# A planned attention stage: costs and delays of the plan set anew, GpSimd and VectorE kept apart in it, one chain of squarings on ScalarE

## The chip, the cores and the metric

The kernel runs on one core of a Trainium2 chip. The metric is the device time of one execution in microseconds, the median of several runs. The engines are TensorE (PE in the rows; PEld is its loading of weights), VectorE (DVE), ScalarE (ACT), GpSimd (POOL) and SyncE (SP), whose queue issues most DMAs. Each engine works through its own queue in order and waits on semaphores for the others.

## The reference

Three stages follow each other. The first is a recurrence over 768 positions, for 2 batches of 8 heads with head size 48:

```python
scale = np.minimum(mag, 0.999) / (mag + 1e-06)          # mag = |a_re + i a_im|
for t in range(S):
    new_re = ar * S_re - ai * S_im                      # ar, ai: scaled a at t
    new_im = ar * S_im + ai * S_re
    S_re, S_im = new_re + kv, new_im                    # kv = outer(k_t, v_t)
    y[:, :, t] = np.einsum('bhd,bhde->bhe', q[:, :, t], S_re)
```

Its output, 1536 tokens of 384 numbers, goes through a routed layer: `x @ w_gate`, the largest of 8 logits picks an expert, each expert takes tokens up to a capacity in their order, computes `relu(x @ w1) @ w2`, and the result is multiplied by the softmax weight. The third stage is a feed-forward layer with 2048 hidden units and a leaky ReLU with a learned slope for each unit. All in float32.

## The kernel before

The recurrence is turned into attention over tiles of 128 positions, 12 tiles (6 for each batch), numbered `i`. A tile's decay is computed in logarithms: `log_polar(i)` (L388) makes the logarithm of the magnitude, `l`, and the tangent of the angle, `t`, by a chain that goes back and forth between ScalarE (Ln, Exp, Square, `w`) and VectorE (L403, L415, L422). `decay(i)` (L429) sums `l` over the positions with a matmul with a triangle (L436, `pl`), and takes the exponentials `ar` = exp(pl/8) (L438) and `ai` = exp(-pl/8) (L439) on ScalarE. Each is then squared three times in place, which gives the eighth power: `times(e, n, key)` (L378), with the engine of each squaring from the table `DOUBLE`. Before, all 72 squarings (12 tiles, `ar` and `ai`, three times) are on GpSimd (L384). `edge(i)` (L444) turns the last row of `ar` with TensorE (L458, `pz`) into the factor `ezs` by which the state decays (VectorE copies at L467 and L471). `turns(i)` (L475) sums the angles (L484, L487, `pt`) and reduces them (`r`, `f`); `rotate(i)` (L510) makes sines and cosines `cs` (L520, L535; L527 on VectorE), scales `q` and `k` with `ar` and `ai` (L542), and turns them (L547, `qq` and `kk`). `attend(i)` (L552) transposes them with TensorE (L572), evicts them on ScalarE (L577, `kT`, `qT`), multiplies them (L591, `sc`), masks the scores on VectorE (L597, `pT`), and sums `y` from the scores and values (L606) and from the state `Z` (L610). The state is renewed with `u` (L623) by two VectorE instructions, L649 and L656. ScalarE evicts the output of the tile (L642, `x`). `route(g)` (L664) transposes `x`, computes the logits and, with some 20 small VectorE instructions for two or three tiles at a time (L708 to L752), the rows to which GpSimd scatters `x` by an indirect DMA (L761).

ScalarE holds one table of functions at a time: table 6 for `log_polar` and `decay`, table 9 for `turns` and `rotate`. `stage(s, ...)` changes it for a group of one or two tiles, so table loads (L349) alternate through the stage. A squaring isn't bound to a table in the plan; the order has 15 table loads before and in the change.

The order of the whole stage comes from a planner, `Plan` (L68). Each step is entered with an engine, a cost in microseconds, the values that it uses and writes, and a lag after which its result can be used. `order()` (L100) lays the steps on a clock of its own, always the step that can start first, with ties by rank; the steps are then emitted in that order, and `emit` chains the instructions of each engine in it. So the costs and lags set an order for each queue (SP's included), and the times on the chip follow from the waits in it. Before, the costs were `C_ACT` 0.52, `C_TT` 0.6, `C_STT` 0.62 and so on, the lag 0.06 (TensorE 0.24), and the planner knew nothing of the ports of VectorE and GpSimd.

During the stage the two weight blocks of the first expert are loaded and split in a high and a low part (`whole`, L865; ScalarE L881, VectorE L885). Behind the stage come `first_expert`, `finish_routes`, and the experts: `ffn` (L988) computes a hidden block `hp` of 128 units (L1011, nine matmuls), ScalarE and VectorE make `gh` and `gl` of it (L1019, L1020), and the block's share of `y` follows (L1001, six matmuls). `unit` (L250) brings in the next expert's weights in pieces: a DMA to `st` (L283), `wh` on ScalarE (L287), `wl` on VectorE (L288). This part isn't planned; its order comes from the compiler's scheduling.

Of the kernel before, what the change touches and what calls it, by code (L numbers as in the profile page):

```python
# [16 lines left out]
ALU = mybir.AluOpType  # L17
# [31 lines left out]
EVICT = 'AAAA'  # L49
DOUBLE = (('GGG', 'GGG'),) * NTL  # L50
TURN = 'AV' * 6
ABS = 'V' * NTL
C_ACT, C_BIAS, C_TT, C_STT, C_PS, C_WIDE, C_SQ = 0.52, 0.61, 0.6, 0.62, 0.56, 1.0, 1.0
SLACK = 0.02
# [13 lines left out]
class Plan:  # L68
# [8 lines left out]

    def op(self, engine, cost, fn, use=(), put=(), new=(), after=(), lag=0.06):
        n = len(self.ops)
        deps = set(after)  # L80
        for v in use:
            if v in self.writer:
                deps.add(self.writer[v])
            self.readers.setdefault(v, []).append(n)
        for v in put:
            if v in self.writer:
                deps.add(self.writer[v])
            deps.update(self.readers.get(v, ()))
        for v in put:
            self.writer[v], self.readers[v] = n, []  # L90
        for tag, v in new:
            self.tagged[v] = tag
        for v in set(use) | set(put):
            if v in self.tagged:
                self.users.setdefault(v, []).append(n)
        deps.discard(n)
        self.ops.append(dict(engine=engine, cost=cost, fn=fn, deps=deps, new=list(new), lag=lag, rank=self.rank))
        return n

    def order(self):  # L100
# [20 lines left out]
        while ready:  # L121
            best = []
            for i in ready:
                o = ops[i]
                t = max([free.get(o["engine"], 0.0)] + [done[d] for d in o["deps"]])
                ok = True
                need = {}
                for tag, _ in o["new"]:
                    need[tag] = need.get(tag, 0) + 1
                for tag, k in need.items():  # L130
                    if len(slots[tag]) < k or (tag not in self.loose and queue[tag][0] != i):
                        ok = False
# [54 lines left out]
def tile_kernel(  # L187
# [144 lines left out]
    def vector(cost, fn, **kw):  # L332
        return plan.op("V", cost, fn, **kw)
# [4 lines left out]
    def tensor(cost, fn, **kw):  # L338
        return plan.op("T", cost, fn, lag=0.24, **kw)

# [37 lines left out]
    def times(e, n, key):  # L378
        def fn():
            t = tl[key]  # L380
            if e == "A":
                A(out=t, in_=t, func=ACTF.Square)
            else:
                (V if e == "V" else G).tensor_tensor(out=t, in0=t, in1=t, op=ALU.mult)  # L384

        plan.op(e, {"A": C_ACT, "V": C_TT, "G": C_SQ}[e], fn, use=[key], put=[key])

    def log_polar(i):  # L388
# [13 lines left out]
        scalar(C_ACT, lambda: A(out=t2(), in_=t1(), func=ACTF.Exp, scale=-1.0), True, use=[l], put=[t], new=[("t2", t)])  # L402
        vector(C_TT, lambda: V.tensor_tensor(out=t2(), in0=t2(), in1=tl[f"ai{i}"], op=ALU.mult), use=[t, f"ai{i}"], put=[t])  # L403

        def square():
# [4 lines left out]

        plan.op(SQUARE[i], {"A": C_ACT, "V": C_TT, "G": C_SQ}[SQUARE[i]], square, use=[t], put=[w], new=[("t3", w)])
        scalar(C_ACT, lambda: A(out=t3(), in_=t3(), func=ACTF.Ln, bias=1.0), True, use=[w], put=[w])
        vector(
            C_STT,
            lambda: V.scalar_tensor_tensor(out=t1(), in0=t3(), scalar=0.5, in1=t1(), op0=ALU.mult, op1=ALU.add),  # L415
            use=[w, l], put=[l],
        )
# [4 lines left out]
            lambda: V.scalar_tensor_tensor(out=t1(), in0=t1(), scalar=LN999, in1=t3(), op0=ALU.min, op1=ALU.subtract),  # L422
            use=[w, l], put=[l],
        )
# [19 lines left out]
    def edge(i):  # L444
# [15 lines left out]
        def spread():  # L460
# [5 lines left out]
        tensor(0.26, turn, use=[e0, "ident"], put=[p], new=[("pc", p)])  # L466
        vector(0.15, lambda: V.tensor_copy(out=ze(), in_=pz()[:, :, 31]), use=[p], put=[f"ze{i}"])  # L467
        tensor(0.2, spread, use=[f"ze{i}", "cst"], put=[p])
        vector(
            0.15,  # L470
            lambda: V.tensor_copy(out=ezs[:, i, :].rearrange("p (j c) -> p j c", c=2), in_=pz()[:, :, 32:34]),  # L471
# [38 lines left out]
    def rotate(i):  # L510
# [11 lines left out]
        if ABS[i] == "A":  # L522
            scalar(C_ACT, lambda: A(out=cs()[:, :, 0, :], in_=fv(), func=ACTF.Abs), use=[f"f{i}"], put=[c_])
        else:
            vector(
                0.4,
                lambda: V.tensor_scalar(  # L527
                    out=cs()[:, :, 0, :].bitcast(U32), in0=fv().bitcast(U32), scalar1=0x7FFFFFFF, scalar2=None,
                    op0=ALU.bitwise_and,
                ),  # L530
                use=[f"f{i}"], put=[c_],
            )
# [5 lines left out]
        for dst, e, s, c in (("kk", "ai", "k", ck), ("qq", "ar", "q", cq)):  # L538
# [9 lines left out]

            vector(C_STT, scaled, use=[ek, sk], put=[ek])
            vector(C_WIDE, turned, use=[ek, c_], put=[dk], new=[(dst, dk)])  # L550

    def attend(i):  # L552
# [12 lines left out]
        def tr(hh):  # L565
            for src, nm, sc in ((kk, "kT", 1.0 / LAM), (qq, "qT", 1.0)):
# [15 lines left out]
                e = EVICT[2 * hh + (nm == "qT")]  # L582
                plan.op(e, {"A": 0.6, "V": 0.68}[e], evict, use=[p], put=[t])

        def scores(hh):
# [13 lines left out]
            tensor(0.9, dots, use=[f"kT{i}{hh}", f"qT{i}{hh}"], put=[p], new=[("sc", p), ("pT", t)])  # L599
            vector(0.7, mask, use=[p], put=[t])  # L600

# [41 lines left out]

        scalar(0.5, out, use=[f"y{i}"], put=[f"x{i}"], new=[("x", f"x{i}")])
        if not last:
            zv = Z[:, 0:DM].rearrange("p (h d) -> p h d", d=D)
            vector(
                0.56,
                lambda: V.scalar_tensor_tensor(  # L649
# [4 lines left out]
            vector(  # L654
                0.6,
                lambda: V.tensor_tensor(  # L656
                    out=zv, in0=zv, in1=ezs[:, i, :].unsqueeze(2).to_broadcast([96, H, D]), op=ALU.mult
                ),
                use=[zk, f"ez{i}"], put=[zk],
            )  # L660
# [3 lines left out]
    def route(g):  # L664
# [11 lines left out]
        for j, i in enumerate(tl_):  # L676
# [188 lines left out]
    def whole(kk):  # L865
# [5 lines left out]
        for j in range(c // m):  # L871
# [399 lines left out]
```

## Time and profile before

| | us |
|---|---|
| median of 3 runs | 592.74 (592.65 to 595.22) |
| the profiled execution | 592.36 |
| its span, first to last instruction | 590.6 |
| TensorE busy | 527.0 (89%) |
| VectorE busy | 356.2 (60%) |
| ScalarE busy | 308.5 (52%) |
| GpSimd busy | 110.7 (19%) |

The span is shorter than the execution by what lies around the first and the last instruction. An engine's busy time is the time with an instruction in execution; instructions of one engine overlap a little, so the sum of their durations is larger. The granted clock is the share of TensorE's full clock that it was given: 1.0 is 2.4 GHz, 0.5 is 1.2 GHz, and a value between is a mean over a stretch with both. A wait is put down to the engine and line whose result came last.

### The profile page before, as it was taken

How to read it: one execution, taken by the hardware profiler on the slowest of the kernel's cores; microseconds unless marked ns; L12 is line 12 of the kernel's file. 1: busy time of each engine (PE TensorE's matmuls, PEld its weight loads, DVE VectorE, ACT ScalarE, POOL GpSimd, SP SyncE). 2: the span in 40 equal slices, each digit the busy share in tenths (PEclk: the TensorE clock that was granted, in tenths of full speed). 3: DMA queues.
4: the chain of work that ended last, by engine and by line, in shares of the span. 5: the costliest groups of instructions: out<-in, count | busy, mean ns of one | idle time of the engine just before them, and what ended most of it. 6: DMA issues, size and time to landing. Idle time of an engine off the chain costs nothing.

```text
span 590.6 us, 8614 instructions
## 1 busy us (share of the span) xinstructions
PE 527.0 (89%) x3270; PEld 483.3 (82%) x3270; DVE 356.2 (60%) x617; ACT 308.5 (52%) x565; POOL 110.7 (19%) x119
## 2 busy tenths in 40 slices
PE   1677969796898968799999999899999999999996
PEld 0466869795888868799999998688899999989986
DVE  2558798869638431677765796979783333333322
ACT  6577866675334231666655643446464443453433
POOL 2518084708027221000000003030200000000000
PEclk9967998899798798899999999999999999999999
DMA  8994334201000108888768746435400000010001
GB/s 281 354 344 147 95 94 139 89 14 42 0 28 1 55 29 136 275 260 257 253 205 322 234 148 222 161 130 156 149 20 35 22 0 1 0 54 2 0 2 53
DMA packets 37407, 71.01 MB, mean 120 GB/s; under 512 B 4105, under 2 KB 30098, under 8 KB 36594
## 3 DMA queue, kind: packets, MB, share of 16 engines
q1 hardware_dynamic: 35570, 65.30, 34.3%
q0 software_dynamic: 1792, 5.12, 2.5%
q8 instruction: 27, 0.44, 0.3%
q14 instruction: 18, 0.15, 0.1%
HBM read 55.84 MB, written 14.56 MB: 119 GB/s over the span
## 4 chain that ended last, share of the span: by engine, by line
PE 75%; DVE 9%; DMA 6%; POOL 3%; ACT 3%; issue 2%; SPq 0%; POOLq 0%; ACTq 0%; DVEq 0%
PE hp L1011 26%; PE y L1001 26%; PE sc L591 5%; PE y L606 4%; PE y L610 3%; DMA st<-in_moe_w 2%; PE pt L484 2%; POOL ai L384 2%; PE pkT L572 2%; DVE Z L656 2%; PE u L623 1%; POOL ar L384 1%; PE pt L487 1%; DMA gs_d<-gate,sidx 1%; PE pt L983 1%
## 5 line engine op out<-in xcount | busy, mean ns | idle before, releaser
L1011 PE MATMUL hp<-xh,wh 128*128 128x256 f32 (+1 forms) x336 | 112.5, 335 | 3.1 <-PEq L1060 2.9
L1001 PE MATMUL y<-wh,gh 128*128 128x384 f32 x320 | 109.7, 343 | 4.9 <-ACT gh L1019 4.9
L1011 PE MATMUL hp<-xl,wh 128*128 128x256 f32 (+1 forms) x336 | 111.9, 333 | 0.6 <-DVE xl L1188 0.6
L1011 PE MATMUL hp<-xh,wl 128*128 128x256 f32 (+1 forms) x336 | 111.9, 333 | 0.0
L1001 PE MATMUL y<-wl,gh 128*128 128x384 f32 x320 | 107.9, 337 | 0.0
L1001 PE MATMUL y<-wh,gl 128*128 128x384 f32 x320 | 89.3, 340 | 0.2 <-DVE gl L1020 0.2
L288 DVE TENSOR_TENSOR wl<-st,wh 128x768 fp32r<-128x768 f32 (+1 forms) x63 | 67.4, 1070 | 31.3 <-ACT wh L287 30.7
L287 ACT ACTIVATE wh<-st 128x768 fp32r<-128x768 f32 (+1 forms) x63 | 58.9, 935 | 30.6 <-DMA st<-in_moe_w 18.1
L1026 DVE SCALAR_TENSOR_TENSOR gn<-gn,nalp,gp 128x512 f32<-128x512 f32 x48 | 35.9, 748 | 62.7 <-ACT gp L1025 62.7
L1011 PEld LDWEIGHTS hp<-xh,wh 128*128 128x128 f32 x336 | 64.5, 192 | 8.6 <-issue 3.0
L1011 PEld LDWEIGHTS hp<-xl,wh 128*128 128x128 f32 x336 | 64.6, 192 | 5.7 <-DVE xl L1188 1.0
L1011 PEld LDWEIGHTS hp<-xh,wl 128*128 128x128 f32 x336 | 64.6, 192 | 5.0
L1001 PEld LDWEIGHTS y<-wh,gh 128*128 128x128 f32 x320 | 60.6, 189 | 7.4 <-ACT gh L1019 5.6
L1024 ACT ACTIVATE gn<-hp 128x512 f32<-128x512 f32 x48 | 28.7, 597 | 71.5 <-PE hp L1011 60.5
L1001 PEld LDWEIGHTS y<-wl,gh 128*128 128x128 f32 x320 | 60.5, 189 | 1.2
L1001 PEld LDWEIGHTS y<-wh,gl 128*128 128x128 f32 x320 | 56.9, 189 | 1.2 <-DVE gl L1020 0.7
L1028 DVE TENSOR_TENSOR gl<-gn,gh 128x512 fp32r<-128x512 f32 x48 | 33.1, 690 | 29.5 <-ACT gh L1027 29.4
L384 POOL TENSOR_TENSOR ar<-ar 128x384 f32<-128x384 f32 x36 | 35.2, 977 | 77.1 <-ACT ar L438 77.0
L1019 ACT ACTIVATE gh<-hp 128x256 fp32r<-128x256 f32 x64 | 24.2, 380 | 45.3 <-PE hp L1011 45.3
L606 PE MATMUL y<-vt,pT 128*128 128x128 f32 x192 | 38.8, 297 | 7.0 <-DVE pT L597 7.0
L1027 ACT ACTIVATE gh<-gn 128x512 fp32r<-128x512 f32 x48 | 30.2, 630 | 22.3 <-DVE gn L1026 21.1
L384 POOL TENSOR_TENSOR ai<-ai 128x384 f32<-128x384 f32 x36 | 40.1, 1114 | 0.0
(166 smaller groups left out, 869.3 us busy)
## 6 DMA issues: line engine op xcount, KB each, us to landing
st<-in_moe_w SPq DMA_DIRECT2D x24, 512.0 KB, 4.6
st<-in_moe_w SPq DMA_DIRECT2D x32, 384.0 KB, 3.6
sw<-in_moe_w_in SPq DMA_DIRECT2D x6, 1024.0 KB, 6.2
sw<-in_moe_w_out SPq DMA_DIRECT2D x8, 768.0 KB, 4.3
xs_d<-zero SPq DMA_DIRECT2D x1, 4608.0 KB, 15.4
ys_d<-o SPq DMA_DIRECT2D x16, 192.0 KB, 2.7
rows<-xs_d SPq DMA_DIRECT2D x14, 192.0 KB, 4.6
ar<-in_a_re SPq DMA_DIRECT2D x12, 192.0 KB, 3.8
```

The lines of the kernel that those rows point to most:

```text
L287: follow(A(out=wh[:, js], in_=st, func=ACTF.Copy), behind, "A")
L288: ins = eng[j].tensor_tensor(out=wl[:, js], in0=st, in1=wh[:, js].bitcast(F32), op=ALU.subtract)
L384: (V if e == "V" else G).tensor_tensor(out=t, in0=t, in1=t, op=ALU.mult)
L591: T.matmul(out=sc[:, h, :], lhsT=tl[f"kT{i}{hh}"][:, h, :], rhs=tl[f"qT{i}{hh}"][:, h, :], start=True, stop=True)
L606: T.matmul(out=y()[:, o:o + P], lhsT=tl[f"pT{i}{hh}"][:, h, :], rhs=tl[vk][:, o:o + P], start=True, stop=(c == 0))
L1001: T.matmul(out=ys[t], lhsT=a[:, sl], rhs=b[:, f, :], start=(ft == 0 and m == 0), stop=(ft == nf - 1 and m == 2))
L1011: ins = T.matmul(out=hp, lhsT=a[:, c, fs], rhs=b[:, c, :], start=(n == 0), stop=(n == 3 * KC - 1))
L1019: last["A"] = A(out=gh, in_=hp, func=ACTF.Relu)
L1024: A(out=gn, in_=hp, func=ACTF.Relu, scale=-1.0)
L1026: V.scalar_tensor_tensor(out=gn, in0=gn, scalar=nalp[:, ft:ft + 1], in1=gp, op0=ALU.mult, op1=ALU.add)
L1027: last["A"] = A(out=gh, in_=gn, func=ACTF.Copy)
L1028: last["V"] = V.tensor_tensor(out=gl, in0=gn, in1=gh.bitcast(F32), op=ALU.subtract)
```

## The change

Twelve tiles' `ar` are squared on ScalarE instead of GpSimd (`DOUBLE`), three squarings each; `ai` stays on GpSimd. The costs of the plan get other values, most of them smaller, and the lag gets one value for each engine (`LAG`). A step can be marked `port`: the planner then keeps it apart in time from all other steps so marked, as if they shared an engine. Marked are the squarings on GpSimd and the VectorE steps with two operands in SBUF, and a few more. No instruction is added or left out; but for the 36 squarings, none changes its engine. The core of the diff (left out are the other marks and costs of the same kind):

```diff
-DOUBLE = (('GGG', 'GGG'),) * NTL
+DOUBLE = (('AAA', 'GGG'),) * NTL
...
-C_ACT, C_BIAS, C_TT, C_STT, C_PS, C_WIDE, C_SQ = 0.52, 0.61, 0.6, 0.62, 0.56, 1.0, 1.0
+C_ACT, C_BIAS, C_TT, C_STT, C_PS, C_WIDE, C_SQ = 0.415, 0.51, 0.47, 0.5, 0.47, 0.87, 0.79
+LAG = {'A': 0.14, 'V': 0.13, 'G': 0.1, 'T': 0.28, 'S': 2.2}
...
-    def op(self, engine, cost, fn, use=(), put=(), new=(), after=(), lag=0.06):
+    def op(self, engine, cost, fn, use=(), put=(), new=(), after=(), lag=None, port=False):
         n = len(self.ops)
+        lag = LAG[engine] if lag is None else lag
...
-                t = max([free.get(o["engine"], 0.0)] + [done[d] for d in o["deps"]])
+                t = max([free.get(o["engine"], 0.0), free.get("port", 0.0) if o["port"] else 0.0] + [done[d] for d in o["deps"]])
...
             free[o["engine"]] = t + o["cost"]
+            if o["port"]:
+                free["port"] = t + o["cost"]
...
-        plan.op(e, {"A": C_ACT, "V": C_TT, "G": C_SQ}[e], fn, use=[key], put=[key])
+        plan.op(e, {"A": C_ACT, "V": C_TT, "G": C_SQ}[e], fn, use=[key], put=[key], port=e != "A")
...
-            vector(C_STT, scaled, use=[ek, sk], put=[ek])
-            vector(C_WIDE, turned, use=[ek, c_], put=[dk], new=[(dst, dk)])
+            vector(0.53, scaled, use=[ek, sk], put=[ek], port=True)
+            vector(C_WIDE, turned, use=[ek, c_], put=[dk], new=[(dst, dk)], port=True)
...
-                plan.op(e, {"A": 0.6, "V": 0.68}[e], evict, use=[p], put=[t])
+                plan.op(e, {"A": 0.49, "V": 0.6}[e], evict, use=[p], put=[t])
...
-            vector(0.7, mask, use=[p], put=[t])
+            vector(0.6, mask, use=[p], put=[t])
...
-        scalar(0.5, out, use=[f"y{i}"], put=[f"x{i}"], new=[("x", f"x{i}")])
+        scalar(0.39, out, use=[f"y{i}"], put=[f"x{i}"], new=[("x", f"x{i}")])
...
-            scalar(0.95, high, use=[key], put=[f"h{key}"])
-            vector(1.05, low, use=[key, f"h{key}"], put=[f"l{key}"])
+            scalar(0.74, high, use=[key], put=[f"h{key}"])
+            vector(0.9, low, use=[key, f"h{key}"], put=[f"l{key}"], port=True)
```

What this does to the queues is shown at three places. In the rows a name carries its tile (`ar8` is `ar` of tile 8) and behind it the number of its buffer; x3 marks three instructions alike. Lines of the changed kernel stand four to six higher than those of the one before.

GpSimd, tiles 8 to 11, before (`ar` and `ai` in turn, the scatters L761 of three output tiles between; tile 9 goes on so for four more rows, and tiles 10 and 11 follow in the same way, with two scatters ahead of them):

```order
L384 TENSOR_TENSOR ar8_596<-ar8_596 128x384
L761 DMA xs_d_82<-x_975,sidx_78 3072x384
L761 DMA xs_d_82<-x_1126,sidx_78 3072x384
L761 DMA xs_d_82<-x_1230,sidx_78 3072x384
L384 TENSOR_TENSOR ai8_585<-ai8_585 128x384
L384 TENSOR_TENSOR ar8_596<-ar8_596 128x384
L384 TENSOR_TENSOR ai8_585<-ai8_585 128x384
L384 TENSOR_TENSOR ar9_661<-ar9_661 128x384
L384 TENSOR_TENSOR ai9_639<-ai9_639 128x384
```

and in the change:

```order
L388 TENSOR_TENSOR ai8_613<-ai8_613 128x384 x3
L767 DMA xs_d_82<-x_922,sidx_78 3072x384
L767 DMA xs_d_82<-x_1129,sidx_78 3072x384
L767 DMA xs_d_82<-x_1237,sidx_78 3072x384
L388 TENSOR_TENSOR ai9_634<-ai9_634 128x384 x3
L767 DMA xs_d_82<-x_1423,sidx_78 3072x384
L767 DMA xs_d_82<-x_1535,sidx_78 3072x384
L388 TENSOR_TENSOR ai10_962<-ai10_962 128x384 x3
L388 TENSOR_TENSOR ai11_1009<-ai11_1009 128x384 x3
```

Nine squarings stood in one run between the scatters; now three do, and six where there were twelve.

ScalarE in the first half of the stage, the decay of tile 4 beside the logarithms of tiles 6 and 7, before:

```order
L407 ACTIVATE w7_716<-t7_696 128x384
L418 ACTIVATE w6_683<-l6_646 128x384
L438 ACTIVATE ar4_167<-pl4_702 128x384
L419 ACTIVATE w6_683<-w6_683,bk_69 128x384
L439 ACTIVATE ai4_175<-pl4_702 128x384
L412 ACTIVATE w7_716<-w7_716 128x384
L577 ACTIVATE kT30_747<-pkT30_727 96x512
```

and in the change (L386 is the squaring):

```order
L444 ACTIVATE ar4_168<-pl4_662 128x384
L418 ACTIVATE w6_676<-w6_676 128x384
L445 ACTIVATE ai4_176<-pl4_662 128x384
L583 ACTIVATE kT21_698<-pkT21_682 96x512
L583 ACTIVATE qT21_705<-pqT21_688 96x512
L386 ACTIVATE ar4_168<-ar4_168 128x384
L691 ACTIVATE xT1_722<-px1_707 128x384
L424 ACTIVATE w6_676<-l6_642 128x384
L386 ACTIVATE ar4_168<-ar4_168 128x384
L425 ACTIVATE w6_676<-w6_676,bk_69 128x384
L386 ACTIVATE ar4_168<-ar4_168 128x384
L406 ACTIVATE t7_736<-l7_664 128x384
```

The three squarings of a tile stand between the evictions `kT`, `qT`, `xT` and the chain `w` of the tiles ahead.

ScalarE at the start of the first expert, behind the plan, before:

```order
L1019 ACTIVATE gh_2841<-hp_2831 128x256
L1019 ACTIVATE gh_2861<-hp_2851 128x256
L287 ACTIVATE wh2_2845<-st2_2847 128x1024
L1019 ACTIVATE gh_2903<-hp_2893 128x256
L1019 ACTIVATE gh_2927<-hp_2917 128x256
L287 ACTIVATE wh2_2845<-st2_2889 128x1024
L287 ACTIVATE wh2_2845<-st2_2913 128x1024
```

and in the change:

```order
L1025 ACTIVATE gh_2841<-hp_2831 128x256
L291 ACTIVATE wh2_2845<-st2_2847 128x1024
L1025 ACTIVATE gh_2861<-hp_2851 128x256
L1025 ACTIVATE gh_2903<-hp_2893 128x256
L291 ACTIVATE wh2_2845<-st2_2889 128x1024
L291 ACTIVATE wh2_2845<-st2_2913 128x1024
L1025 ACTIVATE gh_2927<-hp_2917 128x256
```

The first piece of the next expert's weights (`wh2`) stands one place further ahead, in front of the second hidden block.

## Rows read from the trace of the kernel before

**Rows 1.** Busy time by stretch: us, each engine's busy us (instructions), PE clock, DMA share, GB/s

```profile
10.70:130.00 119.30, 95.58 (x627) 82.33 (x628) 86.66 (x154) 82.55 (x156) 54.60 (x51) 0.87 0.50 170
130.00:216.00 86.00, 74.15 (x555) 67.30 (x554) 52.34 (x129) 36.48 (x68) 31.73 (x35) 0.88 0.06 22
149.00:155.00 6.00, 5.97 (x30) 5.70 (x31) 1.49 (x4) 1.53 (x3) 0.00 (x0) 0.53 0.00 0
189.00:199.00 10.00, 9.26 (x46) 8.45 (x47) 6.21 (x23) 1.93 (x4) 0.93 (x1) 0.50 0.00 1
250.00:400.00 150.00, 146.78 (x996) 141.88 (x996) 112.16 (x172) 81.60 (x150) 10.96 (x9) 1.00 0.66 218
```

The engines stand in the order PE, PEld, DVE, ACT, POOL.

**Rows 2.** Groups by form, GpSimd and ScalarE, 0 to 222 us: busy us, mean ns

```profile
L384 POOL TENSOR_TENSOR ai<-ai 128x384 f32<-128x384 f32 x36 | 40.1, 1114 | 0.0
L384 POOL TENSOR_TENSOR ar<-ar 128x384 f32<-128x384 f32 x36 | 35.2, 977 | 77.1 <-ACT ar L438 77.0
L407 ACT ACTIVATE w<-t 128x384 f32<-128x384 f32 x12 | 6.2, 518 | 3.5 <-DVE t L403 3.5
```

**Rows 3.** Groups by form, VectorE, 0 to 222 us

```profile
L656 DVE TENSOR_TENSOR Z<-Z,ezs 96x384 f32<-96x384 f32 x10 | 13.5, 1346 | 0.1
L718 DVE CAST ocb<-racc 128x8 bf16<-128x8 f32 x12 | 3.7, 307 | 0.2
```

**Rows 4.** Timeline around 140 to 149 us: start, duration, engine, line

```profile
140.41 0.85 POOL L384 TENSOR_TENSOR ai<-ai 128x384 f32<-128x384 f32 x1
146.68 0.81 POOL L384 TENSOR_TENSOR ai<-ai 128x384 f32<-128x384 f32 x1
140.75 7.16 DVE L656 TENSOR_TENSOR Z<-Z,ezs 96x384 f32<-96x384 f32 x1
149.03 0.80 PE L606 MATMUL y<-vt,pT 128*128 128x128 f32 x2 [5.30 <-DVE pT L597]
```

**Rows 5.** Timeline, VectorE at 158 and 182 us, TensorE behind the latter

```profile
158.48 0.61 DVE L542 SCALAR_TENSOR_TENSOR ai<-k,cst,ai 128x384 f32<-128x384 f32 x1
...
160.41 0.95 DVE L547 TENSOR_TENSOR qq<-ar,cs 128x768 f32<-128x768 f32 x1
...
182.15 0.98 DVE L542 SCALAR_TENSOR_TENSOR ar<-q,cst,ar 128x384 f32<-128x384 f32 x1
...
185.65 1.57 DVE L547 TENSOR_TENSOR kk<-ai,cs 128x768 f32<-128x768 f32 x1
...
185.87 0.61 PE L572 MATMUL pqT<-ident,qq 128*96 128x128 f32 x4 [1.71 <-DVE qq L547]
187.37 0.61 PE L572 MATMUL pkT<-ident,kk 128*96 128x128 f32 x4 [0.56 <-DVE kk L547]
```

**Rows 6.** TensorE's waits, 10.7 to 130 us: total, times, longest

```profile
PE pz L458 <- POOL ar L384: 9.0, 4, 4.6
PE pqT L572 <- ACT kT L577: 3.6, 1, 3.6
PE sc L591 <- ACT qT L577: 3.4, 3, 2.0
PE pp L726 <- DVE ocb L718: 2.5, 1, 2.5
PE pqT L572 <- ACT qT L577: 2.2, 1, 2.2
```

**Rows 7.** Timeline, two ScalarE instructions of the same shape, back to back

```profile
36.04 0.51 ACT L479 ACTIVATE t<-t 128x384 f32<-128x384 f32 x1
36.45 0.51 ACT L520 ACTIVATE cs<-f 128x384 f32<-128x384 f32 x1
```

**Rows 8.** Timeline, ScalarE: output of the last tile, first weight piece

```profile
211.67 0.49 ACT L642 ACTIVATE x<-y 128x384 f32<-128x384 f32 x1 [3.75 <-PE y L610]
...
229.66 1.06 ACT L287 ACTIVATE wh<-st 128x1024 fp32r<-128x1024 f32 x1 [4.32 <-DMA gs_d<-gate,sidx]
```

**Rows 9.** TensorE's waits, 220 to 262 us

```profile
PE y L1001 <- ACT gh L1019: 4.9, 3, 3.0
```

More of the change, by code (lines that the diff above doesn't have):

```diff
@@ L96, in op @@
         deps.discard(n)
-        self.ops.append(dict(engine=engine, cost=cost, fn=fn, deps=deps, new=list(new), lag=lag, rank=self.rank))
+        self.ops.append(dict(engine=engine, cost=cost, fn=fn, deps=deps, new=list(new), lag=lag, rank=self.rank, port=port))
         return n
@@ L338, in tensor @@
     def tensor(cost, fn, **kw):
-        return plan.op("T", cost, fn, lag=0.24, **kw)
+        return plan.op("T", cost, fn, **kw)
     def scalar(cost, fn, table=False, **kw):
@@ L402, in log_polar @@
         scalar(C_ACT, lambda: A(out=t2(), in_=t1(), func=ACTF.Exp, scale=-1.0), True, use=[l], put=[t], new=[("t2", t)])
-        vector(C_TT, lambda: V.tensor_tensor(out=t2(), in0=t2(), in1=tl[f"ai{i}"], op=ALU.mult), use=[t, f"ai{i}"], put=[t])
+        vector(C_TT, lambda: V.tensor_tensor(out=t2(), in0=t2(), in1=tl[f"ai{i}"], op=ALU.mult), use=[t, f"ai{i}"], put=[t],
+               port=True)
         def square():
@@ L409, in square @@
                 (V if SQUARE[i] == "V" else G).tensor_tensor(out=t3(), in0=t2(), in1=t2(), op=ALU.mult)
-        plan.op(SQUARE[i], {"A": C_ACT, "V": C_TT, "G": C_SQ}[SQUARE[i]], square, use=[t], put=[w], new=[("t3", w)])
+        plan.op(SQUARE[i], {"A": C_ACT, "V": C_TT, "G": C_SQ}[SQUARE[i]], square, use=[t], put=[w], new=[("t3", w)],
+                port=SQUARE[i] != "A")
         scalar(C_ACT, lambda: A(out=t3(), in_=t3(), func=ACTF.Ln, bias=1.0), True, use=[w], put=[w])
@@ L415, in log_polar @@
             lambda: V.scalar_tensor_tensor(out=t1(), in0=t3(), scalar=0.5, in1=t1(), op0=ALU.mult, op1=ALU.add),
-            use=[w, l], put=[l],
+            use=[w, l], put=[l], port=True,
         )
@@ L422, in log_polar @@
             lambda: V.scalar_tensor_tensor(out=t1(), in0=t1(), scalar=LN999, in1=t3(), op0=ALU.min, op1=ALU.subtract),
-            use=[w, l], put=[l],
+            use=[w, l], put=[l], port=True,
         )
@@ L466, in edge @@
         tensor(0.26, turn, use=[e0, "ident"], put=[p], new=[("pc", p)])
-        vector(0.15, lambda: V.tensor_copy(out=ze(), in_=pz()[:, :, 31]), use=[p], put=[f"ze{i}"])
+        vector(0.08, lambda: V.tensor_copy(out=ze(), in_=pz()[:, :, 31]), use=[p], put=[f"ze{i}"])
         tensor(0.2, spread, use=[f"ze{i}", "cst"], put=[p])
         vector(
-            0.15,
+            0.08,
             lambda: V.tensor_copy(out=ezs[:, i, :].rearrange("p (j c) -> p j c", c=2), in_=pz()[:, :, 32:34]),
@@ L525, in rotate @@
             vector(
-                0.4,
+                0.27,
                 lambda: V.tensor_scalar(
@@ L530, in rotate @@
                 ),
-                use=[f"f{i}"], put=[c_],
+                use=[f"f{i}"], put=[c_], port=True,
             )
@@ L647, in attend @@
             vector(
-                0.56,
+                0.47,
                 lambda: V.scalar_tensor_tensor(
@@ L654, in attend @@
             vector(
-                0.6,
+                0.47,
                 lambda: V.tensor_tensor(
@@ L658, in attend @@
                 ),
-                use=[zk, f"ez{i}"], put=[zk],
+                use=[zk, f"ez{i}"], put=[zk], port=True,
             )
@@ L694, in route @@
             tensor(0.34, turn, use=[f"x{i}"], put=[p], new=[("tr", p), ("xT", x)])
-            scalar(0.5, evict, use=[p], put=[x])
+            scalar(0.39, evict, use=[p], put=[x])
             tensor(
@@ L754, in place @@
                 late.extend([sl, st["lg"]])
-        vector(1.1 + 0.3 * n, choose, use=[f"lg{g}", "racc", "ready"], put=["racc", f"oc{g}"])
+        vector(1.2 + 0.25 * n, choose, use=[f"lg{g}", "racc", "ready"], put=["racc", f"oc{g}"])
         tensor(0.3, count, use=[f"oc{g}", "ready"], put=[f"pp{g}"], new=[("y" if tail else "u", f"pp{g}")])
-        vector(1.3, place, use=[f"pp{g}"], put=[f"si{g}"])
+        vector(2.0 if tl_[0] < CHT else 1.3, place, use=[f"pp{g}"], put=[f"si{g}"])
         for i in tl_:
@@ L772, in scatter @@
                 scatters.append(ins)
-            pool(1.2, scatter, use=[f"si{g}", f"x{i}", "zeroed"], put=[f"xs{i}"], lag=2.0)
+            pool(1.2, scatter, use=[f"si{g}", f"x{i}", "zeroed"], put=[f"xs{i}"], lag=2.0, port=False)
     early = []
```

## The prediction, made before the changed kernel ran

> **What bounds the kernel now.** I read the busy time by stretch first [rows 1]. The span falls into the attention stage (to about 216 us) and the expert and feed-forward stages behind it. From 250 us TensorE is busy 146.78 of 150 us at the full clock: nothing that this change touches can be won there, and all that is won or lost earlier shifts it as a block. In the attention stage no engine is full. From 10.7 to 130 us TensorE is busy 95.58 of 119.3 us, VectorE 86.66, ScalarE 82.55; from 130 to 216 us TensorE 74.15 of 86. Its granted clock is 0.87 and 0.88, so about a quarter of the time it stood at 1.2 GHz instead of 2.4. The stage is bound by waits, and by the slow clock that follows them.
>
> What the waits come from shows in three views. GpSimd's squarings, 72 in 75.3 us [rows 2], take 0.78 us each where nothing meets them (nine in a row from 140.41 to 147.5, [rows 4]) but 0.98 and 1.11 us on average. VectorE pays for the same meetings: the rescaling of the state, L656, takes 1346 ns on average and once 7.16 us [rows 3, 4], and L718, a copy of 128x8, 307 ns. The waits of TensorE [rows 6] name GpSimd's `ar` first.
>
> **The change part by part.** My sum is made against the profiled execution, 592.36 us, which is the median of the runs (592.74) within 0.1%.
>
> *GpSimd gives up 36 squarings and meets VectorE less.* Three places of the trace price this.
>
> First place, 140 to 155 us. L656 starts at 140.75 while GpSimd runs nine squarings back to back and ends with the ninth; TensorE waits 5.30 us for the mask queued behind it on VectorE, and then runs from 149 to 155 us at a clock of 0.53 though busy for 5.97 us [rows 1, 4]: 0.47 x 6 = 2.8 us lost. Together 8.1 us. In the new order the longest run that can meet this step is the three squarings of `ai9` between two groups of scatters, 3 x 0.78 = 2.3 us. **I take 6 us won, between 0 and 8.1.** The Trainium skill's page "SBUF — State Buffer", section "Who interferes with whom", says that the pair of ports which the two engines share is locked for one whole instruction and the loser waits until that one ends. By that rule L656 would have lost at most one squaring, 0.8 us, and this term would be about 1 us instead of 6; the row of 7.16 us disagrees, the wait lasted nine instructions.
>
> Second place, 182 to 199 us. The scaling and turning of one tile, two L542 and two L547, takes from 158.48 to 161.36 us where GpSimd rests and from 182.15 to 187.22 where it squares [rows 5]: 2.2 us more. TensorE waits 1.71 and 0.56 us for the two results [rows 5], and from 189 to 199 us runs at a clock of 0.50 while busy 9.26 us [rows 1]: 4.6 us lost. Together 6.9 us. The new order has six squarings of tiles 10 and 11 here where there were twelve. **I take 4 us, between 0 and 6.9.**
>
> Third place, 10.7 to 130 us [rows 6]. TensorE waits 9.0 us for `ar` from GpSimd; 4.6 of it is the first wait, at the start, where a ScalarE table load now stands between the squarings of tile 0, so I leave it as it is. The other 4.4 us end when ScalarE does the chain: three squarings in place of six. Then 3.6 + 3.4 + 2.2 us for `kT` and `qT` (ScalarE stands before them because VectorE is late with `t` and `l`) and 2.5 us for `ocb`, the small copy that GpSimd slows. That is 16.1 us. What replaces a removed wait is the next late input, so **I take half, 8 us, between 0 and 16.1.**
>
> *ScalarE gains 36 squarings.* The square that it already does on this shape, L407, takes 0.52 us [rows 2], and it starts such instructions 0.41 us apart [rows 7]. Of the 36, 24 (tiles 0 to 7) lie before 130 us: 24 x 0.41 = 9.8 us, in a stretch where ScalarE is idle 119.3 - 82.55 = 36.8 us. The other 12 (4.9 us) lie where it is idle 86 - 36.48 = 49.5 us and TensorE is what counts: I cost them at nothing, covered by that idle time; without this cover they cost up to 4.9 us. For the 24 the cover is thinner. ScalarE's queue is served in order and the new order puts them between the evictions `kT`, `qT` and the chain `w`; every one that is ready late holds back an eviction that TensorE waits for. **I take half, 4.9 us lost, between 0 and 9.8.**
>
> *New costs and ports in the plan* are no work of their own; they move instructions, and their effect is in the terms above. On SP's queue the load of `k4` comes earlier, and `vt0`, which waits for the products of tile 0, now stands ahead of `ar6` and `ar7`. ScalarE reads `ar6` only behind the output of tile 1 in either order: a whole tile's products cover it, so nothing. The squarings issue no DMA.
>
> *The first expert.* Code behind the plan moves a little too: on ScalarE the first weight piece `wh2` now comes right behind the first `gh`, ahead of the second. That piece waits for its DMA until 229.66 us [rows 8]. Before, TensorE had 39 matmuls of L1011 and 12 of L1001 in front of the first that needs a `gh` behind the piece; now 34 and 6. The 11 matmuls are done after the wait instead of before it, at 146.78/996 = 0.147 us each [rows 1]: **1.6 us lost**, at least 0 if the pieces land sooner; at most the waits for `gh` there, 4.9 us [rows 9], double.
>
> The sum: -6 - 4 - 8 + 4.9 + 1.6 = -11.5 us, so 592.4 - 11.5 = **580.9 us**. With every gain whole and no loss it would be 592.4 - 31.1 = 561; with no gain and the losses whole, 592.4 + 9.8 + 4.9 = 607.
>
> **The rivals.** A difference below 0.5% (3 us) is about what a measurement of this kernel cannot tell from none.
>
> *The clock comes back as well: 570 us.* In the first stretch 23.7 us of waiting go with 0.13 x 119.3 = 15.5 us of lost clock, 0.65 us for each. If 8 us of waits go there, 5 us of clock go too, and with the first two places whole the sum is -8.1 - 6.9 - 13.2 + 4.9 + 1.6 = -21.7. For it: the two later places show that the slow clock follows a wait. Against it: a replaced wait brings it back.
>
> *The plan sets an order, not times: 592 us.* The separation of GpSimd from VectorE exists only on the planner's clock, which has no slow TensorE in it. If the queues drift apart as they do now, the meetings stay, only half as many squarings take part: half of 6, 4 and 8 is won, 9.0, against 4.9 + 1.6 lost, and 2 to 3 us of that gain is given back to new waits. Then the change does not do what it says, and the time stays within the bound.
>
> *ScalarE becomes the bound of the first stretch: 600 us.* Its 36.8 us of idle time there are themselves waits for VectorE and TensorE. If they stay, all 9.8 us of squarings go onto the path; with 0.65 us of clock for each that is 16.2 us, plus 1.6 us at the first expert, against the 10 us of the two later places: +7.8 us. It needs the third place to give nothing. It turns the sum slower by over 3 us once more than (10 - 1.6 + 3)/1.65 = 6.9 of the 9.8 us are on the path. For it: ScalarE is busy 82.55 of 119.3 us and would be at 92. The Trainium skill's page "Perfetto Trace Analysis", section "Tensor Engine Instruction (MATMUL, LD_WEIGHTS)", notes that ScalarE serves its queue strictly in order, the rule by which a squaring in front of an eviction delays it. Against it: three squarings on ScalarE are 1.2 us, and six on GpSimd were 4.7 us before the tile could go on.
>
> **How the numbers follow.** The forecast, 573 to 588 with the halves moved a third either way, gets 0.50; the returning clock (below 573) 0.15; the order without the times 0.17; ScalarE as the bound 0.18. So faster 0.65, same 0.17, slower 0.18. The range runs from 568 to 599: it takes in the forecast, the second rival, about half of the first and of the third, and leaves out some 0.17.
>
> **What would show it.** Right: GpSimd's mean squaring near 0.8 to 0.9 us with 36 of them; L656 without a row over 3 us; the waits for `ar` on GpSimd gone from TensorE's list but for the first; the output of the last tile, L642 at 211.67 us now [rows 8], some 13 us earlier, and the first expert's wait for `gh` 1 to 2 us longer. Wrong: ScalarE with under 20 us idle up to 130 us and TensorE's waits for `kT` and `qT` grown (third rival); VectorE's L542 and L547 as long as now on average (second rival).

## The result, and the profile after

The changed kernel takes 560.93 us (median of 4 runs, 560.01 to 563.08), the kernel before beside it on the same chip 593.49 us. The ratio is 0.945, with a 95% interval of 0.942 to 0.949. It is faster, as forecast, but by 32 us instead of 11.5: below the range. The profiled execution is the one of 560.01 us, with a span of 558.2 us.

Where the 32.4 us of span come from shows in the busy time by stretch, cut about where the first matmul of the first expert starts (221.68 us before, 187.05 after). The columns are those of [rows 1]. The changed kernel:

```profile
0.00:187.00 187.00, 156.13 (x1192) 137.33 (x1192) 125.14 (x306) 139.31 (x273) 54.94 (x69) 0.96 0.41 135
187.00:558.20 371.20, 356.04 (x2078) 332.15 (x2078) 211.26 (x311) 182.37 (x328) 17.99 (x15) 0.99 0.39 123
```

The kernel before, cut in the same place:

```profile
0.00:222.00 222.00, 171.93 (x1195) 151.46 (x1196) 144.72 (x306) 126.86 (x237) 91.84 (x105) 0.88 0.34 114
222.00:590.60 368.60, 355.11 (x2078) 331.85 (x2076) 211.52 (x311) 181.65 (x328) 18.90 (x15) 0.99 0.39 124
```

By these rows the attention stage is 35.0 us shorter and the rest 2.6 us longer. In the stage, TensorE runs the same matmuls (1195 and 1192 records) in 156.13 us instead of 171.93: 15.8 us less busy time, while its granted clock rises from 0.88 to 0.96. Its idle time falls from 50.1 to 30.9 us: 19.2 us less. So the gain has two parts of similar size: waits, and clock.

It arises on both sides of the output of tile 5 (125.4 us before, 109.21 after). The next four rows are the same view, from 10.7 us to that output and on to the output of tile 11; first the kernel before:

```profile
10.70:125.40 114.70, 90.98 (x591) 78.35 (x592) 83.61 (x148) 78.78 (x147) 54.60 (x51) 0.87 0.52 175
125.40:211.67 86.27, 75.56 (x566) 68.58 (x565) 53.82 (x122) 37.19 (x72) 30.73 (x34) 0.88 0.07 24
```

and the changed kernel:

```profile
10.70:109.21 98.51, 84.50 (x597) 71.83 (x596) 72.55 (x151) 87.99 (x173) 27.96 (x27) 0.95 0.62 203
109.21:175.02 65.81, 64.44 (x559) 59.41 (x557) 45.18 (x120) 40.12 (x81) 20.08 (x22) 1.00 0.09 31
```

Tiles 0 to 5 gain 16.2 us: 9.7 us of TensorE's idle time and 6.5 us of busy time. Tiles 6 to 11 gain 20.5 us: 9.3 us of idle time and 11.1 us of busy time. (Six more matmuls lie in the first stretch than before and seven fewer in the second, so the parts are good to about 1 us.) In tiles 6 to 11 TensorE is now idle 1.4 us of 65.8, at the full clock. ScalarE is nearly full in the first stretch, 87.99 of 98.51 us (78.78 of 114.70 before).

TensorE's waits of the changed kernel from 10.7 to 130 us (total us, times, longest), those for the results named in [rows 6]; there is none for `kT` and none for `ocb`:

```profile
PE pz L464 <- ACT ar L386: 10.1, 3, 4.5
PE sc L597 <- ACT qT L583: 0.9, 1, 0.9
PE pqT L578 <- ACT qT L583: 0.7, 1, 0.7
```

The waits for `kT`, `qT` and `ocb`, 11.7 us in [rows 6], are down to 1.6. The wait for `ar` did not go: 10.1 us for ScalarE's `ar`, where it was 9.0 for GpSimd's; three of them, for tiles 0 to 2. Here ScalarE did hold TensorE up. The timeline of tile 1 (start, us, engine, line; rows between are left out):

```profile
24.08 0.52 ACT L386 ACTIVATE ar<-ar 128x384 f32<-128x384 f32 x1
27.47 0.52 ACT L412 ACTIVATE w<-t 128x384 f32<-128x384 f32 x1 [2.87 <-DVE t L407]
27.90 0.51 ACT L386 ACTIVATE ar<-ar 128x384 f32<-128x384 f32 x1
...
29.14 0.51 ACT L386 ACTIVATE ar<-ar 128x384 f32<-128x384 f32 x1
29.70 0.38 PE L464 MATMUL pz<-ident,ar 32*96 32x32 f32 x4 [4.06 <-ACT ar L386]
```

The second and third squaring of tile 1 stand in ScalarE's queue behind `w` of another tile, which waits 2.87 us for VectorE's `t`; TensorE waits 4.06 us for the third. At tile 0 a table load of 1.28 us and two other instructions stand between the three squarings, and TensorE waits 4.45 us.

The groups of instructions by form, 0 to 187 us, on VectorE, GpSimd and ScalarE (busy us, mean ns, idle time before):

```profile
L662 DVE TENSOR_TENSOR Z<-Z,ezs 96x384 f32<-96x384 f32 x10 | 6.6, 664 | 0.1
L724 DVE CAST ocb<-racc 128x8 bf16<-128x8 f32 x12 | 2.0, 168 | 0.2
L388 POOL TENSOR_TENSOR ai<-ai 128x384 f32<-128x384 f32 x36 | 34.9, 970 | 75.8 <-ACT ai L445 73.9
L386 ACT ACTIVATE ar<-ar 128x384 f32<-128x384 f32 x36 | 18.9, 524 | 0.1
```

The ten rescalings of the state (shortest, median and longest in ns, first and last start):

```profile
L662 DVE TENSOR_TENSOR Z<-Z,ezs x10: 540/549/1170, 41.6 to 168.4; 96x384 f32<-96x384 f32 x10
```

The rescaling of the state (L656 before, L662 now) fell from a mean of 1346 ns to 664 [rows 3], and `ocb` from 307 to 168. GpSimd's squarings are half as many; the 36 of `ai` that stay take 970 ns instead of 1114 [rows 2].

### The profile page after: what moved, and what is told of

The parts are those of the page before. It is cut to its first block, busy times and chain, and to the rows that moved or that the text cites. A ratio compares the mean times of both kernels' runs of the same rounds, so it can differ in the third digit from the quotient of the medians.

```text
span 558.2 us, 8597 instructions
## 1 busy us (share of the span) xinstructions
PE 512.2 (92%) x3270; PEld 469.5 (84%) x3270; DVE 336.4 (60%) x617; ACT 321.7 (58%) x601; POOL 72.9 (13%) x83
## 4 chain that ended last, share of the span: by engine, by line
PE 58%; DMA 5%; DVE 2%; ACT 1%; issue 0%; SPq 0%; ACTq 0%
PE hp L1017 29%; PE y L1007 28%; DMA st<-in_moe_w 3%; PE pt L989 1%; DMA rows<-ys_d,eidx 1%; DVE wl L292 1%; DMA sw<-in_moe_w_out 1%; ACT wh L291 1%; DMA out<-o 0%; DVE st L283 0%; PE pt L1171 0%; DVE yl L1183 0%; ACT o L1046 0%; DVE st L280 0%; DVE gl L1026 0%
## 5 line engine op out<-in xcount | busy, mean ns | idle before, releaser
L1017 PEld LDWEIGHTS hp<-xh,wh 128*128 128x128 f32 x336 | 64.1, 191 | 10.1 <-issue 3.8
L388 POOL TENSOR_TENSOR ai<-ai 128x384 f32<-128x384 f32 x36 | 34.9, 970 | 75.8 <-ACT ai L445 73.9
L612 PE MATMUL y<-vt,pT 128*128 128x128 f32 x192 | 37.3, 287 | 2.3 <-DVE pT L603 2.2
L1026 DVE SCALAR_TENSOR_TENSOR gl<-hp,gh 128x256 fp32r<-128x256 f32 x64 | 26.7, 420 | 16.0 <-ACT gh L1025 16.0
```

The source lines that it names most:

```text
L612: T.matmul(out=y()[:, o:o + P], lhsT=tl[f"pT{i}{hh}"][:, h, :], rhs=tl[vk][:, o:o + P], start=True, stop=(c == 0))
L1017: ins = T.matmul(out=hp, lhsT=a[:, c, fs], rhs=b[:, c, :], start=(n == 0), stop=(n == 3 * KC - 1))
L1026: last["V"] = V.scalar_tensor_tensor(out=gl, in0=hp, scalar=0.0, in1=gh.bitcast(F32), op0=ALU.max, op1=ALU.subtract)
```

## The experiments

Four theories stood. **Move**: what pays is the move of the squarings (fewer of them on GpSimd beside VectorE, and a shorter chain for `ar`). **Order**: what pays is the order that the new figures in the plan make. **Both**: neither works without the other. **Clock**: whichever of them takes waits away, TensorE's faster clock is a gain of its own. Each time is the median of the runs named; "before" is the kernel before on the same chip.

### Move and order apart

The first two runs cross the parts: the instruction order of one kernel with the engine of the other.

```diff
--- before: e1_engine_only (the plan still counts on GpSimd)
-            if e == "A":
+            if key[:2] == "ar":
                 A(out=t, in_=t, func=ACTF.Square)
--- after: e2_order_only (the plan still counts on ScalarE)
-            if e == "A":
+            if False:
                 A(out=t, in_=t, func=ACTF.Square)
```

> The program order of the kernel before, instruction by instruction, with the 36 squarings of ar issued to ScalarE in the places where GpSimd had them. If the move of these squarings is what pays (shorter chains to the exponentials' products, fewer GpSimd spans that hold VectorE up), it takes 565 to 575 us: at least half of the 32 us. If the plan's order pays, ScalarE gets 36 instructions of 0.52 us, 19 us, at places that nobody chose for it, and the time is 585 to 600 us.

> The program order of the changed kernel with the 36 squarings of ar given back to GpSimd at the same places. If the order pays by itself, 561 to 570 us. If the move pays, GpSimd again has 72 squarings of about 1 us that the order no longer leaves room for: 580 to 600 us.

| | `ar` squared by GpSimd | `ar` squared by ScalarE |
|---|---|---|
| order of before | 591.4 us | e1: 566.7 us, ratio 0.956 (0.951 to 0.961) |
| order of after | e2: 582.2 us, ratio 0.984 (0.980 to 0.989) | 560.9 us, ratio 0.945 (0.942 to 0.949) |

The move alone is worth 25 us, the order alone 9. In the new order the move is worth 21 us, and with the move made the order is worth 6. (The changed kernel was measured at another time, beside 593.5 us for the kernel before; by the ratios the four figures are 26, 9, 23 and 6 us.) The move is the larger part, and they nearly add up. "Both" falls. The stretch up to the first expert in both runs, columns as above; first e1, in the order of before:

```profile
0.00:197.90 197.90, 163.78 (x1194) 143.58 (x1195) 126.81 (x306) 139.75 (x273) 55.07 (x69) 0.93 0.38 128
```

and e2:

```profile
0.00:207.70 207.70, 161.69 (x1195) 142.22 (x1196) 137.62 (x306) 126.54 (x237) 88.88 (x105) 0.93 0.37 122
```

Against before, e1 has 16.0 us less idle time of TensorE and 8.2 us less busy time; e2 has 4.1 and 10.2. (The profiled execution of e1 is its slowest, 569.4 us, and that of e2 its fastest, 577.3, so the two rows stand closer together than the medians.) Which waits the move takes away shows in TensorE's waits of e1 up to 240 us:

```profile
PE pz L458 <- ACT ar L382: 7.0, 3, 4.4
PE sc L591 <- ACT qT L577: 5.0, 6, 2.2
PE pqT L572 <- ACT kT L577: 3.0, 1, 3.0
PE y L606 <- DVE pT L597: 1.3, 2, 1.0
```

Up to the first expert the waits for VectorE's `pT`, `ocb`, `qq` and `kk` fall from 11.8 us before to 1.3 by the move alone. Those for ScalarE's evictions `kT` and `qT` stay, 10.1 us before and 9.4 in e1; they go only with the new order, to 1.8 in the changed kernel.

### The two parts planned

```diff
--- after: e3_plan_gpsimd
-DOUBLE = (('AAA', 'GGG'),) * NTL
+DOUBLE = (('GGG', 'GGG'),) * NTL
--- before: e4_double_old_plan
-DOUBLE = (('GGG', 'GGG'),) * NTL
+DOUBLE = (('AAA', 'GGG'),) * NTL
```

> The new costs, delays and the shared port in the planner, both chains of squarings on GpSimd: the planner knows where they are and orders round them. If better numbers in the plan are most of the gain, 562 to 575 us. If the engine's relief is, 580 to 593 us, since GpSimd and VectorE now have to take turns for 72 squarings in the plan as well.

> The kernel before with its old costs and delays and without the shared port, the squarings of ar on ScalarE and planned there. If the relief of GpSimd is most of the gain, 562 to 572 us. If the plan's numbers are, 583 to 595 us. If both are needed, about the middle, 575 to 583 us.

e3 took 577.3 us (ratio 0.978, 0.972 to 0.984), between its two branches: a plan that has the new figures and 72 squarings on GpSimd gets 14 us by its order, less than half of the change. e4 took 582.3 us (0.985, 0.981 to 0.989), at the top of its middle range. That is 16 us slower than e1, which has the same work on the same engines, in the order that the old plan made for GpSimd. The old plan's figures, given the move, make an order that wastes most of it: the output of tile 5 comes at 130.0 us in e4 and at 114.5 in e1. Which instructions of that order lose it was not followed further.

### Which figure of the plan

```diff
--- after: e5_port_off
-t = max([free.get(o["engine"], 0.0), free.get("port", 0.0) if o["port"] else 0.0] + ...)
+t = max([free.get(o["engine"], 0.0), 0.0] + ...)
--- after: e6_old_costs
-C_ACT, C_BIAS, C_TT, C_STT, C_PS, C_WIDE, C_SQ = 0.415, 0.51, 0.47, 0.5, 0.47, 0.87, 0.79
+C_ACT, C_BIAS, C_TT, C_STT, C_PS, C_WIDE, C_SQ = 0.52, 0.61, 0.6, 0.62, 0.56, 1.0, 1.0
...
--- after: e7_old_delays
-        lag = LAG[engine] if lag is None else lag
+        lag = {'T': 0.24}.get(engine, 0.06) if lag is None else lag
```

(e6 also takes back the single costs that the change altered.)

> The changed kernel with the shared port taken out of the planner: VectorE and GpSimd may be planned beside each other again. If the port is what keeps VectorE from being held up, VectorE's rescaling of Z rises again towards its 1346 ns mean and the time comes to 568 to 580 us. If 36 squarings on GpSimd are few enough not to collide, it stays at 559 to 564 us.

> The changed kernel with the costs of the kernel before; the new delays, the port and the move of the squarings stay. If the durations in the plan are what made the old plan lose most of the move's gain (old plan with the move: 582 us; old order with the move: 567 us), 570 to 582 us. If the delays or the port did, 560 to 566 us.

> The changed kernel with the delays of the kernel before (0.06 us after every instruction, 0.24 after TensorE's). If the delays are what the plan lacked, 570 to 582 us. If the durations or the port are, 560 to 566 us.

e5: 563.9 us (ratio 0.950, 0.945 to 0.954). e6: 564.4 us (0.952, 0.948 to 0.955). e7: 565.6 us (0.953, 0.950 to 0.957). Each lies 3 to 5 us above the changed kernel; only e7's interval is clear of the changed kernel's, and all three came out in the branch in which the figure that was taken back is not what the old plan lacked. No single figure carries the plan's part, though without all three the move gets 582 us (e4). Without the port the rescaling of the state takes 833 ns on average instead of 664, and its longest 1.81 us instead of 1.17: so the port does shorten the rescaling, but what it is worth in time, 3 us, is not clear of noise.

### What the move takes away

```diff
--- before: e8_spare_squares
-            if e == "A":
+            if key[:2] == "ar":
                 A(out=t, in_=t, func=ACTF.Square)
+                if int(key[2:]) >= 3:
+                    G.tensor_tensor(out=zero, in0=zero, in1=zero, op=ALU.mult)
```

> The old order with the squarings of ar on ScalarE, as in the first run of this study (567 us), and behind 27 of them (tiles 3 to 11) GpSimd squares a spare tile of the same size, whose result nobody uses. GpSimd is as busy as before from tile 3 on, the chain of ar is short. If the gain of the move came from GpSimd being out of VectorE's way and out of ai's, the time goes back to 582 to 592 us. If it came from the shorter chain of ar, it stays at 565 to 573 us.

583.8 us (ratio 0.985, 0.981 to 0.990): 17 of the 25 us of e1 are lost again to 27 squarings whose result nobody uses. So most of the move's gain is GpSimd's absence, not the shorter chain of `ar`. GpSimd's own `ai` squarings also queue behind the spare ones, but VectorE waits for `ai` only 0.7 us in e8's stage, while TensorE's waits for VectorE's `pT`, `ocb` and `qq` are 11.4 us longer than in e1: 1.9 us for `ocb` and 1.3 for `qq`, for which e1 has no wait, and for `pT` (total us, times, longest):

```profile
PE y L608 <- DVE pT L599: 9.5, 5, 5.3
```

The timeline of e8 shows the largest case (start, us, engine, line; between the last two GpSimd rows lie five more of the same kind):

```profile
136.78 7.16 DVE L658 TENSOR_TENSOR Z<-Z,ezs 96x384 f32<-96x384 f32 x1
137.22 0.84 POOL L384 TENSOR_TENSOR zero<-zero 128x384 f32<-128x384 f32 x1
138.00 0.83 POOL L386 TENSOR_TENSOR ai<-ai 128x384 f32<-128x384 f32 x1
...
142.71 0.81 POOL L386 TENSOR_TENSOR ai<-ai 128x384 f32<-128x384 f32 x1
...
145.06 0.80 PE L608 MATMUL y<-vt,pT 128*128 128x128 f32 x2 [5.31 <-DVE pT L599]
```

VectorE's rescaling of the state takes 7.16 us again, as in [rows 4], and TensorE waits 5.31 us behind it. Four of the nine squarings beside it work on a tile that has nothing to do with the attention. In e1, without them, the longest rescaling is 0.91 us, and TensorE's waits for `pT` up to the first expert are 1.3 us, where they are 7.0 before and 9.5 in e8. So long a hold comes once in each of these two traces. Where the two engines meet between 74 and 81 us of the kernel before, they take turns: the same rescaling takes 1.17 us there and the squarings beside it mostly 1.14. What decides between a turn and a hold was not found.

### What the clock alone is worth

```diff
--- before: e9_filled_waits
+FILL = {('pqT', 0, 0): 4, ('pqT', 0, 1): 2, ('pz', 2): 8, ('sc', 1, 0): 2, ('sc', 3, 1): 1, ('pz', 7): 5, ('y', 7, 0): 7, ('pqT', 10, 0): 2}
+    def fill(key, out, n=384, m=P):
+        for _ in range(FILL.get(key, 0)):
+            T.matmul(out=out, lhsT=ident[:, 0:m], rhs=cst[:, 0:n], start=True, stop=True)
...
+            fill(("pz", i), pz()[:, :, 0:32], 128, 96)
             for j in range(H // 2):
                 T.transpose(pz()[:, j, 0:32], ...)
```

(and likewise ahead of the turns, scores and products named in the table; the real matmuls overwrite what is filled in).

> The kernel before, with matmuls of constants put on TensorE's queue in front of eight instructions that waited 1.2 to 5.3 us there; each lot is shorter than the wait that it stands before, and the waits' causes stay. If the clock that falls after a wait is on the path, the stretches behind these places (30 to 45, 55 to 60, 115 to 120, 150 to 165 us) show a clock near 1.0 and the time falls by 4 to 12 us, to 580 to 588. If the clock only stretches what waits anyway, or the added matmuls delay others, 590 to 597 us.

587.0 us against 593.2 (ratio 0.990, 0.983 to 0.996): 6 us faster with more to compute, inside the first branch. The stretch up to the first expert:

```profile
0.00:214.69 214.69, 178.96 (x1254) 151.12 (x1255) 143.75 (x306) 127.42 (x237) 91.90 (x105) 0.93 0.35 118
```

The same stretch, the added matmuls alone (only PE and PEld have any):

```profile
0.00:214.69 214.69, 18.48 (x62) 9.76 (x62) 0.93 0.35 118
```

The kernel's own matmuls are busy 178.96 - 18.48 = 160.5 us, 11.4 less than before (the two overlap a little, so this is an estimate), and the clock is 0.93 instead of 0.88. Not every place worked: the fill for `pqT` of tile 0 had itself to wait 3.8 us for its PSUM buffer. What the filling did shows in the clock by stretch (columns as above), e9 first:

```profile
45.00:60.00 15.00, 13.08 (x104) 10.99 (x103) 13.31 (x18) 12.29 (x26) 12.10 (x12) 1.00 0.45 150
110.00:120.00 10.00, 9.46 (x77) 8.44 (x75) 9.19 (x16) 7.72 (x14) 2.54 (x2) 1.00 0.09 23
145.00:160.00 15.00, 14.85 (x102) 13.29 (x101) 9.11 (x23) 6.73 (x12) 0.00 (x0) 0.79 0.00 1
155.00:160.00 5.00, 5.00 (x22) 4.31 (x21) 1.57 (x8) 1.19 (x2) 0.00 (x0) 0.50 0.00 0
```

and before:

```profile
45.00:60.00 15.00, 10.81 (x72) 9.90 (x71) 12.70 (x18) 12.04 (x26) 12.09 (x12) 0.77 0.41 145
110.00:120.00 10.00, 7.37 (x42) 6.96 (x41) 7.95 (x14) 5.90 (x11) 5.05 (x5) 0.68 0.19 60
145.00:160.00 15.00, 10.97 (x74) 10.27 (x75) 10.49 (x16) 4.84 (x8) 2.49 (x4) 0.77 0.00 0
```

From 45 to 60 and from 110 to 120 us the clock came back with the wait filled. Behind the longest wait, at 145 us, it did not: TensorE is busy 14.85 of 15 us instead of 10.97, and the clock is 0.79 against 0.77, with 5 us at 1.2 GHz though TensorE was busy all through them and in 9.86 of the 10 us before. So at these places of the kernel before, a wait on TensorE cost its own length and, at some of them, a stretch at 1.2 GHz behind it; that second cost is on the path. Not every slow stretch stands behind a wait.

### Further along the same way

```diff
--- after: i1_late_v
-DOUBLE = (('AAA', 'GGG'),) * NTL
+DOUBLE = (('AAA', 'VVV'),) * 3 + (('AAA', 'GGG'),) * (NTL - 7) + (('AAA', 'VVV'),) * 4
--- after: i2_no_gpsimd
-DOUBLE = (('AAA', 'GGG'),) * NTL
+DOUBLE = (('AAA', 'VVV'),) * NTL
--- i2: i3_no_gpsimd_filled
+FILL = {('pz', 0): 12, ('pz', 1): 12}
```

> The changed kernel with the squarings of ai on VectorE for the first three and the last four tiles, where VectorE and ScalarE have idle time, and on GpSimd for the five between. If what is left of GpSimd's squarings still lengthens ai's chain at both ends of the stage, 552 to 559 us. If not, 560 to 566 us.

> The changed kernel with all squarings of ai on VectorE: 36 more instructions of about 0.48 us, 17 us, there, and no squaring left on GpSimd. If holding VectorE up is what GpSimd's squarings cost, VectorE's other instructions shorten by about what it takes over, and the time is 552 to 562 us. If VectorE becomes the bound in the stretch from 30 to 130 us, 565 to 580 us.

> The kernel with ai squared on VectorE and ar on ScalarE (555 us), with twelve matmuls of constants, about 2.5 us, on TensorE's queue in front of the transposes of ar in tiles 0 and 1, where it waited 4.5 and 3.8 us. If the clock after a wait is on the path here too, the half-speed stretch from 30 to 40 us ends sooner and the time is 551 to 554 us. If ScalarE or the loads set the pace of that stretch, nothing changes: 554 to 557 us.

i1: 560.2 us (ratio 0.942, 0.937 to 0.948), the same as the changed kernel within the intervals. i2: 554.8 us (0.936, 0.931 to 0.941), just clear of the changed kernel's interval: some 6 us faster, in its first branch. Its VectorE, 0 to 187 us, by form:

```profile
L388 DVE TENSOR_TENSOR ai<-ai 128x384 f32<-128x384 f32 x36 | 19.6, 552 | 2.1 <-ACT ai L445 1.8
L407 DVE TENSOR_TENSOR t<-t,ai 128x384 f32<-128x384 f32 x12 | 6.5, 552 | 6.4 <-ACT t L406 6.4
L662 DVE TENSOR_TENSOR Z<-Z,ezs 96x384 f32<-96x384 f32 x10 | 5.5, 548 | 0.1
```

and the stretch up to its first expert:

```profile
0.00:183.53 183.53, 153.62 (x1192) 136.02 (x1193) 133.48 (x342) 138.57 (x273) 20.37 (x33) 0.97 0.42 138
```

VectorE takes over 19.6 us of squarings and is busy only 8.3 us longer (133.48 against 125.14): the other 11.3 us are what GpSimd's 36 squarings still cost VectorE's other instructions. i3 took 558.5 us (six runs, 552.0 to 561.1; ratio 0.937, 0.932 to 0.942): above both of its branches by the median, and no gain over i2. Up to the first expert it takes 184.0 us, as i2 does (183.5). Of its two waits the first was filled and the second cut from 3.8 to 1.1 us, and the clock from 30 to 40 us stood at 0.66 as in i2: here too a filled wait did not bring the clock back, and the reason is open.

## Why the prediction was wrong

The direction was right, and so was the main cause, GpSimd out of VectorE's way; the sum was a third of the gain. Even the figure for every gain whole and no loss, 561 us, lies above the profiled 560.0, so the sum lacked a term. (The figure for every loss, 607, left out the first expert.) By its steps, on the profiled executions:

- **First and second place, -10 us, bounds 0 and 15.** Tiles 6 to 11 gained 20.5, more than the upper bound. What I saw there went as forecast: no rescaling over 1.17 us, no wait for `qq` or `kk` left. But I priced two places, and took two thirds of each. TensorE's idle time fell by 9.3 us, from 10.7 to 1.4, and the clock's loss went for the whole stretch, not for 16 us of it: 11.1 us less busy time against the 7.4 us in the bounds. The Trainium skill's page "SBUF — State Buffer", section "Who interferes with whom", gives the shared pair to whoever issues first, for that whole instruction; read so, a wait would be one instruction of the other engine. The rescaling's longest of 1.17 us here agrees with that, e8's 7.16 us beside a spare tile does not, as [rows 4] did not.
- **Third place, "I take half, 8 us".** This is the step that failed most plainly. TensorE's idle time up to the output of tile 5 fell by 9.7 us, close to the 8. The argument for the half, that the next late input takes the place of a removed wait, held for `ar` alone (10.1 us where there were 9.0, so my 4.4 us there gave nothing); the waits for `kT`, `qT` and `ocb` lost 10.1 of their 11.7 us, more than half. The size of the waits is thus right in part by luck. What failed is the clock: the sum put it at nothing for this stretch, and it gave back 6.5 us of busy time.
- **ScalarE, +4.9 us.** The place was wrong. I looked for the loss at the evictions, and TensorE's waits for `kT` and `qT` fell from 9.2 to 1.6 us instead of growing. It is the squarings themselves that stood behind other work in ScalarE's queue: 4.45 and 4.06 us of waits for `ar` at tiles 0 and 1, where GpSimd's `ar` had cost 9.0 us in all. What ScalarE cost on balance no run separates. One half of the third rival's sign came, under 20 us idle (12.1 up to 130 us), the other half, longer waits for the evictions, did not.
- **The first expert, +1.6 us.** From the output of tile 11 to the end it is 4.3 us longer (383.2 against 378.9): 2.0 of it before the first expert's first matmul, the rest behind it. The sign was right by luck: the wait for `gh`, where I looked for the loss, is 4.0 us instead of 4.9 [rows 9]. What took the 4.3 us is open.
- **GpSimd's squarings, 0.8 to 0.9 us expected:** 970 ns. The ones that remain still meet VectorE.
- **The rivals.** "The clock comes back" (570 us, 0.15) was the nearest, and its factor was right for the first stretch: 6.5 us of busy time for 9.7 us of idle time is 0.67, against the 0.65 read from the trace before; in the second stretch it is 1.2. It stayed too high since it kept the half and the 4.9 us. "Order, not times" is refuted by the time and by its sign: L542 and L547 went from 793, 750, 1044 and 1006 ns to 683, 656, 949 and 951. But e1, which has no port in its plan, gets most of the gain as well, and the order alone is worth 9 us. "ScalarE becomes the bound" did not happen.

In short, the failed step is the price of the clock. Its loss stood in the stretches' own rows (0.87 and 0.88, [rows 1]) and entered the forecast for two places of 16 us together; TensorE's busy time fell by 17.6 us, where two thirds of the 7.4 us priced are 4.9. That is some 13 of the 21 us by which the forecast fell short. The discounts make the rest: TensorE's idle time fell by 19.1 us, where the terms leave about 8 after the halves and ScalarE's 4.9. That is 11 us more, of which 2.7 went again as the end of the kernel grew by more than forecast. (These shares are estimates from the rows above.)

## What to carry to other kernels

Price a removed wait on TensorE with the slow clock behind it, over the whole stretch that has such waits; here 0.7 to 1.2 us went with each us of waiting. It is no fixed rate: two filled waits, in e9 and i3, brought no clock back. Where VectorE and GpSimd both work on SBUF tiles, GpSimd's cheap-looking instructions are paid by VectorE: give the work to ScalarE while it has idle time, but look at what stands ahead of it in ScalarE's queue (8.5 us of waits at tiles 0 and 1 here), or do it on VectorE itself. And test a planner's change by crossing its parts, the order of one kernel with the engines of the other: planned anew with old figures, the same move kept 9 of its 25 us.

## What the runs showed that was not expected

- GpSimd work, nearly half of it on an unrelated tile, holds a VectorE instruction of 0.55 us for 7.16 us (e8), as long as in [rows 4]; so it is GpSimd's running, not the data, that holds it. It does so once in each of the two traces; from 74 to 81 us of the kernel before, the two engines take turns.
- 18.5 us of added matmul time made the kernel 6 us faster (e9).
- Runs of one and the same kernel differ by the granted clock, but not by it alone. i1's four runs go from 556.6 us at a mean clock of 0.984 to 563.9 at 0.969, in the order of their clocks. e5's go from 560.6 us at 0.984 to 567.0 at 0.970, but its run at 0.965 took 564.7.
- Moving 36 squarings from GpSimd to VectorE (i2) cost VectorE 8.3 us of busy time, where their own durations add up to 19.6.
